# Attention and two feed-forward layers on one core: the fifth pair's scores traced after the fourth pair's output, first loads on two queues, first head's operands moved by engines and second's by DMA

## The chip, the core and the metric

The kernel runs on one core of a Trainium2 chip. The core has a matrix engine (PE), three elementwise engines (DVE, ACT, POOL) and queues that start DMAs; SP's queue (SPq in the rows) does nothing else, ACT's queue can start DMAs too. Every engine and every queue works through its own list of instructions in order and waits where an input or a buffer is not ready. The metric is the device time of one execution in microseconds.

## What is computed

```python
# q, k, v: (4, 8, 576, 64); x: (2304, 512); d_ff = 2048
scores = q @ k.transpose(0, 1, 3, 2) / 8
scores = where(scores >= max(scores) - tau, scores, -1e9)   # per row
attn   = softmax(scores) @ v                                # (4, 8, 576, 64)
x = attn.transpose(0, 2, 1, 3).reshape(2304, 512)
x = (s * relu(x @ w_in) ** 2 + b) @ w_out                   # moe
h = x @ w2_in                                               # moe2
out = (h * tanh(softplus(h))) @ w2_out
```

## The kernel before

**Attention** works on 16 pairs of heads (4 batches of 4 pairs), each in 9 tiles of 128 query rows. `load_raw` reads q, k and v of a pair, 12 DMAs, all on SP's queue. `prep_qk` transposes q or k on PE (5 transposes, line 206), splits it into a rounded part `hi` (ACT, line 210) and a remainder `lo` (DVE, line 211), and puts these into the operand tiles Q, KH[h], KL[h] by `move`: for the first pair with copies on ACT, DVE and POOL (lines 230 to 234), for the others with DMAs on SP's queue (line 228, 12 for a pair). The tiles `hi` and `lo` have one buffer each, so q's parts wait until k's moves have read theirs.

`scores` makes one tile: 4 matmuls (8 for tile 4, which holds rows of both heads) into a tile S, the scaled copy with row minimum on DVE (`ns`, line 258), the exponential on ACT (line 265) and, by the returned function `finish`, the threshold and row sum on DVE (line 269) and the normalisation on POOL (line 279). `weights_t` transposes the normalised rows (T, lines 291 to 300) and copies them out on ACT (`te`, line 302); `product` multiplies them with v (line 313); `split_x` reads the result of a pair out on ACT and DVE (lines 321, 322) and makes it `x[pair]`.

**Order.** `attention` is a generator. Its step k traces the scores of tile k, the preparation of the next pair at tiles 2 and 4, then `weights_t` of tile k - 7, then `product` of the tile before. So x[3], the last output of the first batch, is traced in step 43, after 8 score tiles of the fifth pair (pair 4, counted from 0). `run` calls this generator alone until x[3] exists, with one step of `w1` (the splitting of the first layer's weights from 64 to 32 bits, `split_w`, lines 59 to 72) for every 12 yields. Then it closes the second buffer of S and gives its PSUM to `mm`, the accumulators of `moe1`, and interleaves attention with `moe1(0)`, `moe1(1)` and `moe1(2)` by planned costs; there attention is traced with a priority that puts it 200 places ahead. `moe1(b)` needs x[4b] to x[4b+3]; its groups are lines 405 (matmuls h and y). `moe1(0)` takes its weights from `w1`, through a ring of 5 units. `moe1(3)` runs with the splitting of the second layer's weights (line 59 again), and `moe2` closes the kernel.

The traced order is a priority, not the order of execution: a planner (`schedule_with_timeline_sim=True`) goes through the traced instructions and puts each on its engine's list when its inputs and buffers are ready by its own costs, lowest priority number first.

Of the kernel before, what the change touches and what calls it, by code (L numbers as in the profile page):

```python
# [8 lines left out]
F32 = mybir.dt.float32  # L9
F32R = mybir.dt.float32r  # L10
# [5 lines left out]
P = 128  # L16
# [3 lines left out]
class Fused:  # L20
# [113 lines left out]
    def attn_alloc(self):  # L134
        nc = self.nc
        self.sets = []

        e4 = self.at.tile([P, 1344], F32, name="E4", bufs=1)
        for g in range(3):
            nc.gpsimd.memset(e4[:, g * 640:g * 640 + 64], 0.0)  # L140
        for g in range(2):

            Q = self.at.tile([P, 1216], F32R, name=f"Q{g}", bufs=1)
            nc.gpsimd.memset(Q[:, 576:640].bitcast(F32), 0.0)
            KH = [self.at.tile([P, 576], F32R, name=f"KH{g}{h}", bufs=1) for h in range(2)]

            KL = [self.at.tile([P, 576], F32R, name=f"KL{g}{h}", bufs=1) for h in range(2)]
            for h in range(2):
                nc.gpsimd.memset(KL[h][HALVES[1 - h], :].bitcast(F32), 0.0)
            self.sets.append((Q, KH, KL, e4[:, g * 640:g * 640 + 704]))  # L150
        self.qk = {}
        for n in "qk":
            t = self.qk[n] = self.at.tile([P, 5, 2, 64], F32, name=f"raw{n}", bufs=1)
            nc.gpsimd.memset(t[64:128, 4], 0.0)
        self.vs = []
        for g in range(2):
            t = self.at.tile([P, 2, 5, 64], F32, name=f"rawv{g}", bufs=1)
            nc.gpsimd.memset(t[64:128, 0, 4, :], 0.0)
            nc.gpsimd.memset(t[0:64, 1, 4, :], 0.0)
            self.vs.append(t)  # L160

    def load_raw(self, pr, nm):
        nc = self.nc
        b, p = divmod(pr, self.NP)
        if b >= self.B:
            return
        src = {"q": self.q, "k": self.k, "v": self.v}[nm]
        h2 = src[b, 2 * p:2 * p + 2]
        rem = h2[:, 512:576, :].rearrange("h r d -> r h d")
        if nm == "v":  # L170
            t = self.vs[pr % 2]
            for h in range(2):
                nc.sync.dma_start(t[:, h, 0:4, :], h2[h, 64 * h:64 * h + 512, :].rearrange("(p c) d -> p c d", c=4))
            nc.sync.dma_start(t[0:64, 0, 4, :], h2[0, 512:576, :])
            nc.sync.dma_start(t[64:128, 1, 4, :], h2[1, 0:64, :])
        else:
            t = self.qk[nm]
            nc.sync.dma_start(t[:, 0:4, 0, :], h2[0, 0:512, :].rearrange("(p c) d -> p c d", c=4))
            if nm == "q":
                nc.sync.dma_start(t[:, 0:4, 1, :], h2[1, 0:512, :].rearrange("(p c) d -> p c d", c=4))  # L180
                nc.sync.dma_start(t[0:64, 4, :, :], rem)
            else:


                full = h2[1, 64:576, :].rearrange("(p c) d -> p c d", c=4)
                nc.sync.dma_start(t[64:128, 0:4, 1, :], full[0:64])
                nc.sync.dma_start(t[0:64, 1:5, 1, :], full[64:128])
                nc.sync.dma_start(t[0:64, 0, 1, :], h2[1, 0:64, :])
                nc.sync.dma_start(t[0:64, 4, 0, :], h2[0, 512:576, :])
        self.raws[pr, nm] = t  # L190

# [3 lines left out]
        pool = self.s2p if self.s2p and self.n_s % 2 else self.sp  # L195
        return pool.tile([P, 1024], F32, tag="S", name=name)

    def prep_qk(self, pr, n):


        nc = self.nc
        raw = self.raws.pop((pr, n))
        Q, KH, KL, _ = self.sets[pr % 2]
        tp = self.s_tile(f"tp{n}{pr}")
        for c in range(5):
            nc.tensor.transpose(tp[:, c * 128:c * 128 + 128], raw[:, c].rearrange("p h d -> p (h d)"), self.ident)
        self.load_raw(pr + 1, n)
        hi = self.at.tile([P, 576], F32R, tag="hi", name=f"hi{n}{pr}", bufs=1)
        lo = self.at.tile([P, 576], F32R, tag="lo", name=f"lo{n}{pr}", bufs=1)
        nc.scalar.copy(hi, tp[:, :576])  # L210
        nc.vector.tensor_tensor(lo, tp[:, :576], hi.bitcast(F32), op=ALU.subtract)
        for h, (own, oth) in enumerate((HALVES, HALVES[::-1])):
            for half, t in ((own, hi), (oth, hi if n == "k" else lo)):
                if n == "k":
                    parts = [(KH[h], 0, 576, 0)]
                else:
                    parts = [(Q, 0, 576, 0)] if h == 0 else [(Q, 0, 512, 704), (Q, 512, 576, 128)]
                for dst, a, z, o in parts:
                    self.move(pr, dst[half, a + o:z + o], t[own, a:z], t is hi)
            if n == "k":  # L220
                self.move(pr, KL[h][own, :], lo[own, :], None)

    def move(self, pr, dst, src, early):


        nc = self.nc
        if pr:
            nc.sync.dma_start(dst.bitcast(F32), src.bitcast(F32))
        elif early is None:
            nc.gpsimd.tensor_copy(dst, src.bitcast(F32))  # L230
        elif early and dst.shape[-1] > 64:
            nc.scalar.copy(dst, src.bitcast(F32))
        else:
            nc.vector.tensor_copy(dst, src.bitcast(F32))

# [88 lines left out]
    def attention(self):  # L326

        nc = self.nc  # L330
        N = 9 * self.B * self.NP
        LAG = 7
        for n in "kq":
            self.load_raw(0, n)
        nc.sync.dma_start(self.tau_c, self.tau.partition_broadcast(P))
        nc.sync.dma_start(self.s_c, self.s.partition_broadcast(P))
        nc.sync.dma_start(self.b_c, self.b.partition_broadcast(P))
        self.load_raw(0, "v")
        for n in "kq":
            self.prep_qk(0, n)  # L340
        fin = todo = None
        tes = {}
        for k in range(N + LAG + 2):
            pr, ti = divmod(k, 9)
            if k < N:
                nxt = self.scores(pr, ti)
                if fin:
                    fin()
                fin = nxt
                yield 550  # L350
                if pr + 1 < self.B * self.NP and ti in (2, 4, 8):
                    if ti == 8:
                        self.load_raw(pr + 1, "v")
                    else:
                        self.prep_qk(pr + 1, "kq"[ti // 2 - 1])
                        yield 500
            elif fin:
                fin()
                fin = None
            j = k - LAG  # L360
            if 0 <= j < N:
                prj, ci = divmod(j, 9)
                tnew = self.weights_t(prj, ci)
                yield 550
            if todo:
                tp, tc, te = todo
                tes[tc] = te
                if tc == 4:
                    self.product(tp, 4, (te, te), True, False)
                    yield 490  # L370
                elif tc > 4:
                    self.product(tp, tc - 5, (tes[tc - 5], te), False, tc == 8)
                    yield 970
                if tc == 8:
                    self.split_x(tp)
            todo = (prj, ci, tnew) if 0 <= j < N else None


    def acc(self, name):
# [204 lines left out]
    def run(self, ctx):  # L584
# [8 lines left out]
        m, a = ExitStack(), ExitStack()  # L593
# [16 lines left out]
        k = 0  # L610
        while 3 not in self.x:
            next(att)
            k += 1
            if k % 12 == 0:
                next(w1)

        pro.close()
# [23 lines left out]
        while a_on or m_on:  # L641
            if a_on and (not m_on or (a_done - 5000.0) / a_left <= m_done / m_left):
                with tc.high_priority(offset=200):
                    c = next(att, None)
                a_on = c is not None
                a_done += c or 0
            else:
                c = next(mo, None)
# [23 lines left out]
HALVES = [slice(0, 64), slice(64, 128)]  # L672
# [45 lines left out]
```

## Time and profile before

| | us |
|---|---|
| three runs | 1215.17, 1219.55, 1219.41 (median 1219.41) |
| the profiled execution | 1216.89, its span 1215.1 |
| attention alone, to the first matmul of `moe1(0)` | 131.47 |
| attention with `moe1(0)` | 132 to 356 |
| attention with `moe1(1)` and `moe1(2)` | 356 to 664 |
| `moe1(3)` and the splitting of the second layer | 664 to 830 |
| `moe2` | 830 to 1215 |

A row of a timeline is start, duration, engine, line, operation, written tile <- read tile, shapes and a count; square brackets hold the idle time of the engine before the row and what ended it. Times are microseconds from the first instruction. A row of a table by stretches gives each engine's busy time with the number of its instructions, then the granted clock of PE as a share of full speed.

### The profile page before, as it was taken

To read this page: it belongs to the slowest core of one execution; us is meant where nothing else is said; L and a number is where in the kernel's file an instruction comes from. 1 tells how busy PE (TensorE), PEld (TensorE's weight loads), DVE (VectorE), ACT (ScalarE), POOL (GpSimd) and SP (SyncE) were. 2 spreads that over 40 slices of the span, in tenths; PEclk is the share of its full clock that TensorE was granted. 3 is DMA by queue.
4 is the path that set the end of the run, shared out by engine and by line. 5 is a ranking of instruction groups with operands and counts; after the bars stand their busy time and mean duration, and the time that the engine had idled before them with its cause. 6 is when DMAs were issued, how large, how long until landed. Compare 5 with 4: busy or idle time off the path is not lost.

```text
span 1215.1 us, 20290 instructions
## 1 busy us (share of the span) xinstructions
PE 1153.1 (95%) x7104; PEld 983.9 (81%) x7104; DVE 868.4 (71%) x1585; ACT 592.5 (49%) x1153; POOL 657.9 (54%) x841
## 2 busy tenths in 40 slices
PE   5888999999899999999999999988999999999998
PEld 4666878877788998988998999966888888888886
DVE  5888777878885465664652799799977676767865
ACT  4666666575555544455532575453433333344332
POOL 5566777786644343335431354346755655555654
PEclk8989999999999999999999999989999999999999
DMA  5556466576585445474433898842130020020000
GB/s 129 157 142 180 111 210 183 168 208 175 175 288 165 144 144 165 127 227 132 131 99 111 288 323 267 293 148 70 36 104 1 1 70 1 8 97 1 18 1 35
DMA packets 123671, 161.88 MB, mean 133 GB/s; under 512 B 57392, under 2 KB 78896, under 8 KB 123568
## 3 DMA queue, kind: packets, MB, share of 16 engines
q1 hardware_dynamic: 123568, 160.58, 43.2%
q8 instruction: 56, 0.92, 0.3%
q14 instruction: 47, 0.39, 0.1%
HBM read 107.48 MB, written 30.93 MB: 114 GB/s over the span
## 4 chain that ended last, share of the span: by engine, by line
PE 59%; DVE 13%; DMA 10%; POOL 6%; issue 5%; ACT 4%; SPq 2%; DVEq 0%; ACTq 0%; POOLq 0%
PE o L539 12%; PE h L405 11%; PE y L405 9%; PE pv L313 6%; PE hp L495 6%; PE hm L495 6%; PE S L254 5%; DMA wraw<-in_moe_w_in_dram 5%; PE T L291 4%; DMA wraw<-in_moe_w_out_dram 3%; DVE d L512 3%; POOL e L279 2%; DVE wa L67 2%; DVE wa L68 2%; DVE wa L66 2%
## 5 line engine op out<-in xcount | busy, mean ns | idle before, releaser
L512 DVE RECIPROCAL d<-d 128x512 f32<-128x512 f32 (+1 forms) x80 | 242.0, 3025 | 0.0
L405 PE MATMUL y<-gh,w 128*128 128x288 f32 x768 | 164.0, 299 | 2.7 <-DVE y L452 2.7
L405 PE MATMUL h<-xh,w 128*128 128x288 f32 x768 | 164.8, 300 | 1.3 <-DMA w<-w 1.0
L269 DVE SCALAR_TENSOR_TENSOR e<-ns,st,e 128x576 f32<-128x576 f32 x128 | 120.9, 948 | 45.5 <-ACT e L265 30.1
L260 POOL TENSOR_SCALAR st<-st,tau_c 128x1 f32<-128x1 f32 x144 | 60.9, 424 | 165.9 <-DVE ns L258 151.0
L539 PE MATMUL o<-w2o,g2h 128*128 128x512 f32 x576 | 149.7, 395 | 0.1
L258 DVE TENSOR_SCALAR_CACHE_REDUCE ns<-S 128x576 f32<-128x576 f32 x144 | 107.8, 752 | 55.6 <-PE S L254 54.9
L279 POOL TENSOR_SCALAR e<-e,st 128x576 f32<-128x576 f32 x128 | 126.4, 997 | 31.3 <-DVE st L274 28.9
L405 PEld LDWEIGHTS y<-gh,w 128*128 128x128 f32 x768 | 125.7, 188 | 10.2 <-issue 4.4
L265 ACT ACTIVATE e<-ns,st 128x576 f32<-128x576 f32 x128 | 98.9, 776 | 70.6 <-DVE ns L258 59.5
L405 PEld LDWEIGHTS h<-xh,w 128*128 128x128 f32 x768 | 125.7, 188 | 8.5 <-issue 5.7
L539 PEld LDWEIGHTS o<-w2o,g2h 128*128 128x128 f32 x576 | 107.1, 188 | 24.8 <-ACT g2h L519 0.6
L302 ACT COPY te<-T 128x576 f32<-128x576 f32 x144 | 91.3, 634 | 72.1 <-PE T L296 64.9
L429 POOL TENSOR_TENSOR gl<-rr,gh 128x288 fp32r<-128x288 f32 x96 | 81.0, 850 | 73.8 <-DVE rr L428 63.2
L495 PE MATMUL hp<-y,w2i 128*128 128x512 f32 (+1 forms) x480 | 113.6, 380 | 6.1 <-DVE t L511 6.0
L516 POOL TENSOR_TENSOR t<-t,d 128x512 f32<-128x512 f32 (+1 forms) x80 | 94.9, 1186 | 40.5 <-DVE d L512 40.3
L523 POOL TENSOR_TENSOR g2l<-t,g2h 128x512 fp32r<-128x512 f32 (+1 forms) x80 | 95.5, 1193 | 38.4 <-ACT g2h L519 36.1
L405 PE MATMUL y<-gl,w 128*128 128x288 f32 x384 | 113.7, 296 | 1.5 <-DVE gl L429 1.5
L405 PE MATMUL h<-xl,w 128*128 128x288 f32 x384 | 113.8, 296 | 0.0
L495 PE MATMUL hm<-y,w2i 128*128 128x512 f32 (+1 forms) x480 | 110.1, 373 | 3.1 <-DVE t L511 3.0
L254 PE MATMUL S<-KH,Q 128*128 128x288 f32 x320 | 101.6, 333 | 11.8 <-DVE ns L258 4.0
L291 PE MATMUL T<-ident,e 128*128 128x128 f32 x576 | 99.1, 281 | 13.6 <-ACT te L302 9.3
(100 smaller groups left out, 2481.8 us busy)
## 6 DMA issues: line engine op xcount, KB each, us to landing
w<-w SPq DMA_DIRECT2D x96, 512.0 KB, 4.2
wraw<-in_moe_w_in_dram SPq DMA_DIRECT2D x64, 256.0 KB, 3.9
w<-wp SPq DMA_DIRECT2D x32, 512.0 KB, 4.0
wraw<-in_moe_w_out_dram SPq DMA_DIRECT2D x64, 256.0 KB, 4.3
KH<-hik SPq DMA_DIRECT2D x60, 144.0 KB, 2.5
y<-yT SPq DMA_DIRECT2D x32, 256.0 KB, 4.1
KL<-lok SPq DMA_DIRECT2D x30, 144.0 KB, 2.7
rawq<-in_q_dram SPq DMA_DIRECT2D x32, 128.0 KB, 3.1
```

Of the source, the lines that this page charges most:

```text
L254: nc.tensor.matmul(so, Q[:, c0:c0 + 128], kt[:, ks], start=(i == 0), stop=(i == len(terms) - 1))
L258: nc.vector.tensor_scalar(ns.rearrange("p (h n) -> p h n", h=2), sv, -0.125, 3.0e38, op0=ALU.mult, op1=ALU.min, accum_out=nm[:, c1])
L265: nc.scalar.activation(e, ns, AF.Exp, bias=nm[:, c1], scale=-1.0)
L269: nc.vector.scalar_tensor_tensor(e, ns, nthr[:, c1], e, op0=ALU.is_le, op1=ALU.mult, accum_out=sm[:, c1])
L279: nc.gpsimd.tensor_scalar(t, t, rinv[:, j:j + 1], u[:, j:j + 1], op0=ALU.mult, op1=ALU.add)
L291: nc.tensor.transpose(T[:, i * 128:i * 128 + 128], self.es[pr, i, "pair"][:, o:o + 128], self.ident)
L405: nc.tensor.matmul(acc[:, :n], w[:, wl, c], rhs[c][xl][:, ts], start=(i == 0), stop=(i == 11))
L495: nc.tensor.matmul(hp[:, :n], w[:, wl, kc, fs], yy[kc], start=(i == 0), stop=(i == 11))
L512: nc.vector.reciprocal(d, d)
L516: nc.gpsimd.tensor_tensor(t, t, d, op=ALU.mult)
L523: nc.gpsimd.tensor_tensor(gl, t, gh.bitcast(F32), op=ALU.subtract)
L539: nc.tensor.matmul(outs[t], g[:, t * 128:t * 128 + 128], w[:, wl, fc % 4, :], start=(fc == 0 and i == 0), stop=(fc == 15 and i == 2))
```

## The change

Four things are changed. In `attention`, the scores of pair 4 are not traced until x[3] exists: from tile 36 on (9 tiles by 4 pairs) the loop goes on with `weights_t` and `product` alone, without the lag of 7, until `split_x(3)` is traced, and takes up the scores then; from there the lag of 7 is built up anew. In `load_raw`, for the first pair, the second head's loads of k (3) and q (1) go to ACT's queue. The first pair is prepared by `prep_first`: k and q are transposed one behind the other, q's parts get buffers of their own (tag `te`), the first head's operands are copied by ACT, POOL and DVE, and the second head's (3 for k, 4 for q) are moved by DMAs on SP's queue. The zeroing of the raw tiles moves to the head of POOL's list, and `w1` takes a step for every 16 yields in place of 12.

```diff
 load_raw:
+        other = nc.sync if pr else nc.scalar
...
-                nc.sync.dma_start(t[:, 0:4, 1, :], h2[1, 0:512, :].rearrange("(p c) d -> p c d", c=4))
+                other.dma_start(t[:, 0:4, 1, :], h2[1, 0:512, :].rearrange("(p c) d -> p c d", c=4))
...
-                nc.sync.dma_start(t[64:128, 0:4, 1, :], full[0:64])
-                nc.sync.dma_start(t[0:64, 1:5, 1, :], full[64:128])
-                nc.sync.dma_start(t[0:64, 0, 1, :], h2[1, 0:64, :])
+                other.dma_start(t[64:128, 0:4, 1, :], full[0:64])
+                other.dma_start(t[0:64, 1:5, 1, :], full[64:128])
+                other.dma_start(t[0:64, 0, 1, :], h2[1, 0:64, :])
...
+    def prep_first(self):
+        nc = self.nc
+        tps = [self.raw_t(0, n) for n in "kq"]
+        (kh, kl), (qh, ql) = (self.parts(0, n, tp, tags) for n, tp, tags in
+                              zip("kq", tps, (("hi", "lo"), ("te", "te"))))
+        k0, k1, k2 = self.moves(0, "k", 0, kh, kl)
+        q0, q1 = self.moves(0, "q", 0, qh, ql)
+        nc.scalar.copy(k0[0], k0[1].bitcast(F32))
+        nc.gpsimd.tensor_copy(k1[0], k1[1].bitcast(F32))
+        nc.gpsimd.tensor_copy(k2[0], k2[1].bitcast(F32))
+        nc.scalar.copy(q0[0], q0[1].bitcast(F32))
+        nc.vector.tensor_copy(q1[0], q1[1].bitcast(F32))
+        for n, hi, lo in (("k", kh, kl), ("q", qh, ql)):
+            for dst, src in self.moves(0, n, 1, hi, lo):
+                nc.sync.dma_start(dst.bitcast(F32), src.bitcast(F32))
...
 attention:
-        for k in range(N + LAG + 2):
-            pr, ti = divmod(k, 9)
-            if k < N:
+        s = t = 0
+        while s < N or t < N or todo:
+            on = s < N and not (s == 9 * self.NP and self.NP - 1 not in self.x)
+            if on:
+                pr, ti = divmod(s, 9)
+                s += 1
...
-            j = k - LAG
-            if 0 <= j < N:
-                prj, ci = divmod(j, 9)
-                tnew = self.weights_t(prj, ci)
+            new = None
+            if t < s - LAG or (t < s and not on):
+                prj, ci = divmod(t, 9)
+                t += 1
+                new = prj, ci, self.weights_t(prj, ci)
...
 run:
-            if k % 12 == 0:
+            if k % 16 == 0:
```

`raw_t`, `parts` and `moves` are `prep_qk` cut into three: the transposes with the next pair's load, the two parts, and the list of moves for one head. In `moves` a head of k has three entries (KH twice, KL once), the first head of q two, the second head of q four.

## Rows read from the trace of the kernel before

**Rows 1.** Table of engines on the page: busy us, share of span, instructions.
```profile
PE 1153.1 (95%) x7104; PEld 983.9 (81%) x7104; DVE 868.4 (71%) x1585; ACT 592.5 (49%) x1153; POOL 657.9 (54%) x841
```

**Rows 2.** Busy time by stretches: stretch, length; busy (instructions) of PE, PEld, DVE, ACT, POOL; clock, DMA.
```profile
12.00:101.00 89.00, 73.88 (x426) 54.61 (x427) 73.57 (x206) 50.44 (x88) 54.53 (x73) 0.88 0.58 151
101.00:132.00 31.00, 28.21 (x191) 20.84 (x190) 25.34 (x73) 20.34 (x35) 16.45 (x26) 0.94 0.63 169
132.00:356.00 224.00, 209.26 (x1472) 179.26 (x1470) 176.25 (x439) 136.73 (x287) 160.80 (x227) 0.98 0.63 188
356.00:510.00 154.00, 153.94 (x1147) 139.43 (x1148) 85.18 (x214) 75.63 (x142) 67.33 (x95) 1.00 0.53 158
664.00:830.00 166.00, 154.63 (x1034) 145.00 (x1033) 141.76 (x295) 89.67 (x222) 70.37 (x73) 0.98 0.74 248
```

**Rows 3.** Timeline of the start, all engines.
```profile
4.71 0.63 SPq L180 DMA_DIRECT2D rawq<-in_q_dram  x1
...
5.08 1.30 PE L206 MATMUL tpk<-ident,rawk 128*128 128x128 f32 x5 [5.08 <-DMA rawk<-in_k_dram]
...
7.09 2.71 ACT L232 CAST KH<-hik 64x576 fp32r<-64x576 f32 x4
...
7.92 1.30 PE L206 MATMUL tpq<-ident,rawq 128*128 128x128 f32 x5 [1.54 <-DMA rawq<-in_q_dram]
...
11.52 1.01 DVE L234 CAST Q<-loq 64x576 fp32r<-64x576 f32 x3
...
12.12 0.58 PE L254 MATMUL S<-KH,Q 128*128 128x288 f32 x1 [2.90 <-DVE Q L234]
```

**Rows 4.** Timeline of SP's queue, and of ACT and PE where they wait, 18 to 33 us.
```profile
18.13 0.43 ACT L64 ACTIVATE wraw<-wraw 128x256 f32<-128x256 f32 x1 [2.13 <-DMA wraw<-in_moe_w_in_dram]
...
20.07 1.20 SPq L228 DMA_DIRECT2D KH<-hik  x2
...
27.86 0.61 PE L254 MATMUL S<-KH,Q 128*128 128x288 f32 x1 [1.33 <-DVE loq L211]
...
32.21 1.61 SPq L59 DMA_DIRECT2D wraw<-in_moe_w_in_dram  x3
```

**Rows 5.** View of waits, 0 to 131 us: total, times, longest.
```profile
ACT hiq L210 <- DMA KH<-hik: 0.9, 1, 0.9
```

**Rows 6.** Timeline of PE from the last score tile of pair 3 to `moe1(0)`.
```profile
100.66 0.40 PE L254 MATMUL S<-KH,Q 128*128 128x288 f32 x1
...
103.06 0.40 PE L254 MATMUL S<-KH,Q 128*128 128x288 f32 x1
...
103.69 0.60 PE L291 MATMUL T<-ident,e 128*128 128x128 f32 x4
...
127.33 0.60 PE L291 MATMUL T<-ident,e 128*128 128x128 f32 x4
127.77 0.27 PE L296 MATMUL T<-ident,E 128*128 128x128 f32 x1
127.97 1.19 PE L313 MATMUL pv<-te,rawv 128*64 128x288 f32 x8
129.09 0.40 PE L254 MATMUL S<-KH,Q 128*128 128x288 f32 x1
...
131.47 0.41 PE L405 MATMUL h<-xh,wp 128*128 128x288 f32 x1
```

**Rows 7.** Timeline of ACT, a copy of T in that stretch.
```profile
128.13 0.64 ACT L302 COPY te<-T 128x576 f32<-128x576 f32 x1 [0.39 <-PE T L296]
```

**Rows 8.** Timeline of DVE, one score tile's two passes.
```profile
128.65 0.75 DVE L258 TENSOR_SCALAR_CACHE_REDUCE ns<-S 128x576 f32<-128x576 f32 x1
...
130.60 0.81 DVE L269 SCALAR_TENSOR_TENSOR e<-ns,st,e 128x576 f32<-128x576 f32 x1
```

**Rows 9.** Timeline of POOL, tenth and next splitting of a piece of `w1`.
```profile
97.93 1.19 POOL L72 TENSOR_TENSOR wp<-wa,wp 128x256 fp32r<-128x256 f32 x1 [0.25 <-ACT wp L71]
...
139.04 1.43 POOL L72 TENSOR_TENSOR wp<-wa,wp 128x256 fp32r<-128x256 f32 x2
```

More of the change, by code (lines that the diff above doesn't have):

```diff
@@ L136, in attn_alloc @@
         self.sets = []
+        self.qk = {}
+        for n in "kq":
+            t = self.qk[n] = self.at.tile([P, 5, 2, 64], F32, name=f"raw{n}", bufs=1)
+            nc.gpsimd.memset(t[64:128, 4], 0.0)
         e4 = self.at.tile([P, 1344], F32, name="E4", bufs=1)
@@ L150, in attn_alloc @@
             self.sets.append((Q, KH, KL, e4[:, g * 640:g * 640 + 704]))
[L151 to L154, printed above, removed]
         self.vs = []
@@ L196, in s_tile, with raw_t @@
         return pool.tile([P, 1024], F32, tag="S", name=name)
-    def prep_qk(self, pr, n):
+    def raw_t(self, pr, n):
         nc = self.nc
         raw = self.raws.pop((pr, n))
-        Q, KH, KL, _ = self.sets[pr % 2]
         tp = self.s_tile(f"tp{n}{pr}")
@@ L207, in prep_qk, with parts @@
         self.load_raw(pr + 1, n)
-        hi = self.at.tile([P, 576], F32R, tag="hi", name=f"hi{n}{pr}", bufs=1)
-        lo = self.at.tile([P, 576], F32R, tag="lo", name=f"lo{n}{pr}", bufs=1)
+        return tp
+    def parts(self, pr, n, tp, tags):
+        nc = self.nc
+        hi, lo = (self.at.tile([P, 576], F32R, tag=t, name=f"{w}{n}{pr}", bufs=6 if t == "te" else 1)
+                  for w, t in zip(("hi", "lo"), tags))
         nc.scalar.copy(hi, tp[:, :576])
         nc.vector.tensor_tensor(lo, tp[:, :576], hi.bitcast(F32), op=ALU.subtract)
[L212 to L219, printed above, removed]
-            if n == "k":
-                self.move(pr, KL[h][own, :], lo[own, :], None)
@@ L223, in move, with moves @@
-    def move(self, pr, dst, src, early):
-        nc = self.nc
[L227 to L234, printed above, removed]
+        return hi, lo
+    def moves(self, pr, n, h, hi, lo):
+        Q, KH, KL, _ = self.sets[pr % 2]
+        own, oth = HALVES[h], HALVES[1 - h]
+        out = []
+        for half, t in ((own, hi), (oth, hi if n == "k" else lo)):
+            if n == "k":
+                spans = [(KH[h], 0, 576, 0)]
+            else:
+                spans = [(Q, 0, 576, 0)] if h == 0 else [(Q, 0, 512, 704), (Q, 512, 576, 128)]
+            out += [(dst[half, a + o:z + o], t[own, a:z]) for dst, a, z, o in spans]
+        return out + ([(KL[h][own, :], lo[own, :])] if n == "k" else [])
@@ new lines, in prep_qk @@
+    def prep_qk(self, pr, n):
+        hi, lo = self.parts(pr, n, self.raw_t(pr, n), ("hi", "lo"))
+        for h in range(2):
+            for dst, src in self.moves(pr, n, h, hi, lo):
+                self.nc.sync.dma_start(dst.bitcast(F32), src.bitcast(F32))
+    def prep_first(self):
+        nc = self.nc
+        tps = [self.raw_t(0, n) for n in "kq"]
[11 more added lines that the diff above has]
+                nc.sync.dma_start(dst.bitcast(F32), src.bitcast(F32))
@@ L338, in attention @@
         self.load_raw(0, "v")
-        for n in "kq":
-            self.prep_qk(0, n)
+        self.prep_first()
         fin = todo = None
         tes = {}
-        for k in range(N + LAG + 2):
-            pr, ti = divmod(k, 9)
-            if k < N:
+        s = t = 0
[4 more added lines that the diff above has]
+                s += 1
                 nxt = self.scores(pr, ti)
@@ L375, in attention @@
                     self.split_x(tp)
-            todo = (prj, ci, tnew) if 0 <= j < N else None
+            todo = new
     def acc(self, name):
```

## The prediction

> **What bounds the kernel now.** I read the page's table of engines first: PE is busy for 95% of the span [rows 1], so a change pays only where PE loses time. The busy times by stretches [rows 2] show where that is. With `moe1(1)` PE is busy for 153.94 of 154 us and starts 1147 instructions, one in 0.134 us; time moved into such a stretch comes back one to one. In attention alone it is busy for 73.88 of 89 us with a clock of 0.88 (12 to 101) and for 28.21 of 31 with 0.94 (101 to 132). Here DVE is the fullest engine: 73.57 of 89 and 25.34 of 31. With `moe1(0)` PE still idles for 14.7 of 224 us, and that stretch takes 70 us longer than the next one; DVE is busy for 79% of it. I then read the start row by row [rows 3 to 5], and the end of attention alone [rows 6 to 8].
>
> What a score tile costs: on PE 103.69 - 103.06 = 0.63 us [rows 6] (0.53 more for the tile of both heads), on DVE 0.75 + 0.81 = 1.56 us [rows 8]. What the rest of a tile costs on PE: T from 127.33 to 127.97, 0.64 us, and pv from there to 129.09, 1.12 us [rows 6]. A product is made for 5 of 9 tiles.
>
> **The start.** Before, the transposes of q wait for the load of q's second head, whose issue begins at 4.71 as the seventh of SP's list, and start at 7.92; the first score tile starts at 12.12 and had waited for DVE's three copies of q (11.52, 1.01 us) [rows 3]. Of SP's first eight loads four go to ACT's queue. By SP's 0.63 us for an issue [rows 3], q's second head comes out some 4.71 - 2.6 = 2.1 us earlier, if ACT's queue starts at once. Of the eight copies on ACT and DVE, two by ACT and one by DVE stay: ACT's four for k take 2.71 us, so a copy costs about 0.68. With these together I work out 2.8 us for the first score tile, at 9.3. The zeroing of the raw tiles hides either way, since it was done before the first transposes at 5.08.
>
> Against this stands SP's list. The second head's seven moves are new on it: 7 x 0.6 (KH's two took 1.20 [rows 4]) = 4.2 us, less 4 x 0.63 = 2.5 for the loads that left, a net 1.7 us. They pass in front of pair 1's moves, which were issued from 20.07 on, and of the weights' loads; SP's list is full until the three loads at 32.21 in the timeline. Who waits for that: `hi` has one buffer, so pair 1's `hi` of q waits for its moves of k [rows 5], DVE's `lo` follows it, and at 27.86 a score tile waits for that `lo` 1.33 us, since it needs the S buffer [rows 4]. So the eighth tile hangs on SP's list, not on the first tile's start. Nothing before shows the new order, so I bound it: from 2.8 us gained (SP's moves slip into gaps) to 1.7 lost. I take 1.0 gained, between the ends but nearer to the gain's side, because ACT also loses 2.13 us at 18.13 in waiting for a weight load [rows 4], which the later steps of `w1` may spare.
>
> The Trainium skill speaks against a larger gain ("DMA: Bandwidth & Descriptors", section "Issuing engines are not separate DMA queues"): a second issuing engine saves only the time of initiating, all transfers share the same engines. No row of this trace has loads on two queues; by that rule the 2.1 us above are all that the second queue can give, and the sum stays as it is.
>
> **`w1` for every 16 yields.** Nothing. Its steps in attention alone fall from 9 to 6, but the trace has run ahead of the traced order all along (the tenth piece was split at 97.93, where the traced order had finished some three, and the next only at 139.04 [rows 9]: ten pieces fill the ring of 5 units), so buffers set its pace, and DVE's share of it moves little. If that cover is gone, `moe1(0)` starts with three units where it had five; two units are 48 matmuls, 48 x 0.134 = 6.4 us, which is in the range.
>
> **The end of attention alone.** The last tile of pair 3 starts at 100.66, and `moe1(0)` at 131.47 [rows 6]: 30.8 us. In between stand 11 T, 9 of pair 3 and 2 of pair 2, with 8 products (3 of pair 2, 5 of pair 3), and 11 score tiles: the nine of pair 4 and two of pair 5. Without these, T and te alternate: 0.64 on PE, 0.64 on ACT [rows 7], and about 0.2 between (127.97 to 128.13), which is 1.5 us for a tile without product; with one, pv covers te and a tile takes 0.64 + 1.12 = 1.76. The first two tiles and the last five of pair 3 have one, the other four don't: 7 x 1.76 + 4 x 1.5 = 18.3, and the last product 1.1: 19.4 us. `moe1(0)` so starts 30.8 - 19.4 = 11.4 us earlier. POOL's normalisation of the last four tiles is needed only after six T, some 9 us on, and is done by then.
>
> What leaves this stretch comes back where PE is full: 11 x 0.63 + 0.53 = 7.5 us of scores, ten transposes (the next pair's k and q) at (127.77 - 127.33) / 4 = 0.11, 1.1, and T of (4,0), 0.64 [rows 6]: 9.2 us. The net is 2.2 us gained. PE's loss in the 30.8 us is 30.8 - (11 x 0.64 + 8 x 1.12 + 9.2) = 30.8 - 25.2 = 5.6 us; more than that can't be won here, and it is won if scores fill all gaps of the shorter chain. So the gain is between 0 (nothing moves) and 5.6. I take 2.2, which needs no gap to be filled.
>
> **The restart.** Pair 4 now begins with nothing in flight: nine score tiles go through DVE before its first T. That is 9 x 1.56 = 14.0 us of DVE work, which sat in attention alone, in the stretch with `moe1(0)`, where DVE is busy for 176.25 of 224 us and splits the weights that PE waits for. DVE's idle 48 us hide it, if it lands there; I take 0.5 us lost, and bound it by 0 and by the rival below. x[3] comes 12 us earlier, which is about the time of these nine tiles, so the last output of attention keeps its distance from `moe1(3)`.
>
> **The sum.** 1216.89 - 1.0 - 2.2 + 0.5 = 1214.2 for an execution like the profiled one. That one lies 2.5 us under the median of the runs, 1219.41, so the median would be 1216.7; I put the forecast at 1215, between the two.
>
> **Rivals.** First, the planner undoes the change. The traced order is a priority only: the score tile at 129.09 is one of pair 5, which was traced after x[3], and it ran before it [rows 6]. With 200 places of priority ahead, pair 4's tiles can run amid pair 3's T as they did. Then only the start is left, -1.0: 1215.9, and 1218.4 on the median. Against it: S(4,0) itself, and the rest for as long as the S buffer is taken.
>
> Second, all gaps are filled: the start gives its 2.8 and the chain its 5.6, with nothing lost at the restart: 1216.89 - 8.4 = 1208.5, 1211.0 on the median. For it speaks that ACT and DVE have slack once the scores no longer stand in front.
>
> Third, the other side: DVE paces the stretch with `moe1(0)`. If the nine score tiles, pair 5's preparation (two DVE passes of 0.75) and the rest of what moved, some 17 us, take room at DVE's 79%, the stretch grows by 17 / 0.79 = 21.5 us and not by 9.2: 1216.89 - 1.0 - 11.4 + 21.5 = 1226.0, 1228.5 on the median. It decides from a growth of some 18.5 us on. For it speaks that this stretch is 70 us longer than the next one and PE idles in it; against it that PE is busy in it for 93%.
>
> **Chances.** A difference of 0.5%, 6.1 us, is about what a measurement of this kernel tells from none. The forecast has 0.36, of which 0.06 falls under 1213.3, the bound of faster. The planner undoing it has 0.15, all within 0.5%. All gaps filled has 0.29, faster. DVE pacing the stretch has 0.20, slower. So faster 0.35, within 0.45, slower 0.20. The range takes in most of the second and of the third rival and the unknown ends of the start: 1204 to 1229.
>
> **What would show it.** In the timeline of the start: the first score tile near 9.3 (right) or past 11; the eighth tile before 27 or after 28. At the end of attention alone: `moe1(0)` at 118 to 121, no score tile of pair 4 between the last T of pair 3 for the forecast, and many for the first rival. In the busy times by stretches: `moe1(0)`'s stretch longer by about 9 us. The prediction is wrong if that stretch grows by more than 18, or if PE's clock falls in the thinner chain of T and te, or if the later stretches, which are untouched, move by more than 2 us.

## The result and the profile after

The changed kernel takes 1231.26 us (median of 8, 1225.23 to 1235.29) against 1219.29 beside it: ratio 1.0102, interval 1.0075 to 1.0128. The forecast was 1215.0 in 1204 to 1229, no measurable change; the kernel is slower, and its time lies above the range. The profiled execution took 1228.97 us, its span is 1227.2.

Table of engines of the changed kernel (answers [rows 1]), then its busy times by stretches (columns as in [rows 2]):

```profile
PE 1156.2 (94%) x7104; PEld 988.9 (81%) x7104; DVE 869.3 (71%) x1582; ACT 589.5 (48%) x1149; POOL 661.8 (54%) x841
```

```profile
12.00:101.00 89.00, 72.33 (x419) 54.92 (x420) 71.30 (x203) 50.91 (x87) 54.23 (x72) 0.85 0.62 159
101.00:132.00 31.00, 28.09 (x191) 20.72 (x190) 20.73 (x58) 17.04 (x29) 17.22 (x22) 0.94 0.50 133
132.00:356.00 224.00, 202.09 (x1401) 172.55 (x1399) 177.52 (x431) 131.72 (x282) 157.23 (x224) 0.98 0.59 180
356.00:510.00 154.00, 150.00 (x1100) 134.30 (x1099) 84.06 (x214) 76.56 (x139) 60.25 (x89) 0.99 0.55 164
...
330.00:356.00 26.00, 23.21 (x144) 19.48 (x145) 21.82 (x61) 13.18 (x24) 14.98 (x18) 0.87 0.59 177
356.00:370.00 14.00, 11.19 (x76) 8.32 (x74) 10.95 (x29) 8.42 (x13) 5.59 (x8) 1.00 0.73 212
```

The amount of work is the same; what differs is how much PE has started by a given time. Against [rows 2] it is 7 instructions behind in 12 to 101, level in 101 to 132, 71 behind in 132 to 356 and 47 in 356 to 510: 125 instructions of 0.134 us, 16.8 us, of which 12.1 are left at the end of the span. The two narrow rows show the thickest piece: from 330 to 370 us 220 instructions start. In the kernel before it is 287 (first two rows; the others are x[8] and the handover from `moe1(0)` to `moe1(1)` in the kernel before):

```profile
330.00:356.00 26.00, 25.20 (x180) 20.83 (x178) 23.11 (x60) 14.21 (x25) 9.88 (x13) 1.00 0.88 270
356.00:370.00 14.00, 13.94 (x107) 13.36 (x108) 10.29 (x27) 9.17 (x19) 11.26 (x14) 1.00 0.72 251
...
348.42 0.63 ACT L321 CAST xh<-pv 128x576 fp32r<-128x576 f32 x1
...
351.84 2.47 SPq L397 DMA_DIRECT2D w<-w  x5
...
356.06 0.40 PE L405 MATMUL h<-xh,w 128*128 128x288 f32 x1 [0.44 <-DMA w<-w]
```

Timelines of the changed kernel: the start (answers [rows 3]), the end of attention alone (answers [rows 6]), and the handover from `moe1(0)` to `moe1(1)`, with SP's queue, PE and x[8] (ACT):

```profile
0.72 0.65 ACTq L187 DMA_DIRECT2D rawk<-in_k_dram  x1
...
6.13 1.27 PE L204 MATMUL tpq<-ident,rawq 128*128 128x128 f32 x5
...
9.67 0.82 PE L273 MATMUL S<-KH,Q 128*128 128x288 f32 x2 [2.27 <-DVE Q L250]
...
27.34 0.61 PE L273 MATMUL S<-KH,Q 128*128 128x288 f32 x1
...
108.23 0.40 PE L428 MATMUL h<-xh,wp 128*128 128x288 f32 x1
...
109.93 0.29 PE L273 MATMUL S<-KH,Q 128*128 128x288 f32 x1
...
130.16 0.40 PE L273 MATMUL S<-KH,Q 128*128 128x288 f32 x1
...
132.66 0.64 ACT L340 CAST xh<-pv 128x576 fp32r<-128x576 f32 x1 [0.48 <-PE pv L332]
...
356.75 0.30 PE L428 MATMUL y<-gh,wp 128*128 128x290 f32 x1
...
360.11 0.56 SPq L235 DMA_DIRECT2D Q<-hiq  x1
...
361.74 0.62 ACT L340 CAST xh<-pv 128x576 fp32r<-128x576 f32 x1
...
366.03 0.38 SPq L486 DMA_DIRECT2D yT<-yl  x1
...
367.24 2.83 SPq L420 DMA_DIRECT2D w<-w  x5
...
371.33 0.47 PE L428 MATMUL h<-xh,w 128*128 128x288 f32 x1 [1.19 <-DMA w<-w]
```

The first score tile comes 2.45 us earlier than before, the eighth 0.52. x[3] is read out at 132.66 (131.86 before): seven of pair 4's score tiles (the row at 109.93 is the third, that at 130.16 the last) still run amid pair 3's T, although they are traced behind x[3]. `moe1(0)` has 18 matmuls from 108.23 on and then waits for x[3]. At 350 us `moe1` is hardly behind the kernel before, with 31.0 and 31.7 of its units of 24 matmuls; what is behind is attention: x[8] is read out at 361.74, before at 348.42. At the handover `moe1(1)` starts 14.6 us after the last y of `moe1(0)`: its weight loads (L420, issued from 367.24 on) stand in SP's list behind the loads and moves of an attention pair and the last y's stores. In the kernel before they were issued at 351.84, ahead of those stores, and `moe1(1)` started at 356.06, 4 us after the last y.

PE's waits, 132 to 375 us (total, times, longest), of the changed kernel, then the same three of e3 (the first experiment), the fastest of the kernels below:

```profile
PE S L273 <- DVE ns L277: 9.7, 7, 3.3
PE T L310 <- ACT te L321: 4.4, 7, 1.6
PE T L310 <- POOL e L298: 3.2, 5, 1.1
```

```profile
PE S L273 <- DVE ns L277: 0.6, 1, 0.6
PE T L310 <- ACT te L321: 1.6, 3, 1.1
PE T L310 <- POOL e L298: 0.7, 2, 0.5
```

So PE loses 17.3 us here and 2.9 in e3 to attention's own chain of scores and weights; directly for the pieces of `w1` (`wp`) it waits 2.5 and 1.5 us.

### The profile page after: what moved, and what is told of

It is laid out like the page before. It is cut to its first block, busy times and chain, and to the rows that moved or that the text cites. A ratio compares the mean times of both kernels' runs of the same rounds, so it can differ in the third digit from the quotient of the medians.

```text
span 1227.2 us, 20273 instructions
## 1 busy us (share of the span) xinstructions
PE 1156.2 (94%) x7104; PEld 988.9 (81%) x7104; DVE 869.3 (71%) x1582; ACT 589.5 (48%) x1149; POOL 661.8 (54%) x841
## 4 chain that ended last, share of the span: by engine, by line
PE 60%; DVE 15%; DMA 9%; issue 6%; POOL 6%; ACT 3%; SPq 1%; DVEq 0%; ACTq 0%; POOLq 0%
PE o L562 12%; PE h L428 11%; PE y L428 9%; PE pv L332 6%; PE hp L518 6%; PE hm L518 5%; PE S L273 5%; PE T L310 4%; DMA wraw<-in_moe_w_out_dram 3%; DMA wraw<-in_moe_w_in_dram 3%; DVE d L535 3%; DVE wa L67 2%; DVE wa L68 2%; DVE wa L66 2%; POOL e L298 2%
## 5 line engine op out<-in xcount | busy, mean ns | idle before, releaser
L288 DVE SCALAR_TENSOR_TENSOR e<-ns,st,e 128x576 f32<-128x576 f32 x128 | 117.2, 918 | 47.9 <-ACT e L284 30.4
L298 POOL TENSOR_SCALAR e<-e,st 128x576 f32<-128x576 f32 x128 | 129.8, 1022 | 33.5 <-DVE st L293 29.0
L279 POOL TENSOR_SCALAR st<-st,tau_c 128x1 f32<-128x1 f32 x144 | 57.6, 400 | 155.9 <-DVE ns L277 140.2
L310 PE MATMUL T<-ident,e 128*128 128x128 f32 x576 | 100.0, 282 | 17.3 <-ACT te L321 10.0
```

Of the source, the lines that this page charges most:

```text
L288: nc.vector.scalar_tensor_tensor(e, ns, nthr[:, c1], e, op0=ALU.is_le, op1=ALU.mult, accum_out=sm[:, c1])
L298: nc.gpsimd.tensor_scalar(t, t, rinv[:, j:j + 1], u[:, j:j + 1], op0=ALU.mult, op1=ALU.add)
L310: nc.tensor.transpose(T[:, i * 128:i * 128 + 128], self.es[pr, i, "pair"][:, o:o + 128], self.ident)
```

## The experiments

A stands for: SP's list at the handover is the cause. B: DVE paces the stretch with `moe1(0)`. C: the pace of `w1` starves `moe1(0)`, by its lead (C1, the number of steps before `moe1(0)`) or its density (C2). D: the new first preparation is to blame. R: each edit is first of all another order of the planner's, and the order sets the time. Other letters are explained where they come. Ratios are to the kernel before on the same chip, with 95% intervals. "The order" is the list in which the planner put the instructions of an engine.

**1. One part alone, and the change without its new pace.**

```diff
 e1, attention (the kernel before):
-        for k in range(N + LAG + 2):
+        while s < N or t < N or todo:
+            on = s < N and not (s == 9 * self.NP and self.NP - 1 not in self.x)
...
 e2, attention (the kernel before; with the new load_raw and attn_alloc):
-        for n in "kq":
-            self.prep_qk(0, n)
+        self.prep_first()
```

> The kernel before with the new loop of attention alone (pair 4's scores traced after x[3]); the old first preparation, all first loads on SP, a step of w1 for every 12 yields. Theory A (order of SP's list: moe1(1)'s weight loads stood behind the last y stores of moe1(0), issued at 367.24 us, and cost the 15 us without moe1 work from 356.75 to 371.33): the deferral itself costs little, and since the planner puts these loads in front of the last stores here, the time is 1217 to 1222. Theory B (DVE paces the stretch with moe1(0) after the deferral, rival 3 of the prediction): about 1229 to 1233. Theory C (the pace of w1, 16 in place of 12, is to blame): 1217 to 1221. Theory D (the new first preparation is to blame): 1217 to 1221.

> The kernel before with the new first preparation alone (second queue for four first loads, first head's operands by engines, second head's by DMA); the old loop of attention and 12 yields. Theory A: the first score tile comes 2.4 us earlier and the gain is lost again by pair 0's second head: 1217 to 1220. Theory B and C: the same, 1217 to 1220. Theory D (seven more DMAs on SP's list at the start disturb what follows): 1228 to 1233.

```diff
 run (e3: the changed kernel with the old pace):
-            if k % 16 == 0:
+            if k % 12 == 0:
                 next(w1)
```

> The changed kernel with a step of w1 for every 12 yields again, nothing else. Theory A: the planner puts the first weight loads of moe1(1) ahead of the last y stores of moe1(0) here too, so the gap at the handover closes: 1217 to 1222. Theory B: 1229 to 1233, as DVE has the same work. Theory C: 1217 to 1221, and then the units of moe1(0) lie ahead of those of the changed kernel by 132 us already. Theory D: 1229 to 1233.

Measured: deferral alone 1217.11 us, 0.9992 (0.9971 to 1.0013); first preparation alone 1218.31, 0.9998 (0.9979 to 1.0017); both, with a step for every 12 yields, 1213.49, 0.9959 (0.9941 to 0.9978), which is faster than the kernel before. B and D fall. The forecasts of A and C for e3 were too high, and C's side claim failed: by 130 us e3 has as much of `moe1(0)` as the changed kernel, 0.8 units; at 350 us it has 36.2 units of `moe1` against 31.0. The orders of e1 and e3 are nearly one (laid side by side, 59 of the 7,104 entries of PE's list differ), so their 3.6 us are about what the first preparation is worth in that order: x[3] comes at 126.95 in e3 and 131.3 in e1. Busy times of e3:

```profile
132.00:356.00 224.00, 213.78 (x1505) 183.16 (x1503) 185.27 (x436) 136.32 (x295) 165.54 (x230) 1.00 0.65 201
...
330.00:356.00 26.00, 26.00 (x193) 22.82 (x192) 16.89 (x37) 14.17 (x31) 15.19 (x20) 1.00 0.74 236
```

DVE does more here than in the changed kernel (185.27 against 177.52), and PE starts 104 instructions more: DVE was not full, it stood idle behind others.

**2. The pace with the other parts: the eight combinations.**

```diff
 run (e7: the kernel before; e16: with the deferral; e17: with the first preparation):
-            if k % 12 == 0:
+            if k % 16 == 0:
                 next(w1)
```

> The kernel before with a step of w1 for every 16 yields, nothing else: 7 steps before moe1(0) in place of 9. Theories C1 and C2: slower than before, 1223 to 1231. Theory A (SP's list at the handover is that of the kernel before): 1215 to 1220. Theory E (it is the combination with the deferral, which takes 11 of the 112 yields away, that falls below what moe1(0) needs): 1215 to 1222.

> The kernel before with the new loop of attention alone and a step of w1 for every 16 yields, with the old first preparation: the cell that is missing beside 12 with the deferral (ratio 0.9992) and 16 alone (1.0015). If the loss is one of these two parts together, 1226 to 1233. If all three parts are needed, or by theory R an order of its own: 1213 to 1225.

> The kernel before with the new first preparation and a step of w1 for every 16 yields, with the old loop of attention: the last missing cell of the eight (before 1, deferral 0.9992, first preparation 0.9998, sixteen 1.0015, deferral and first preparation 0.9959, deferral and sixteen 1.0029, all three 1.0102). If the first preparation and sixteen together bring the loss: 1224 to 1233. If only all three do (theory R, an order of its own): 1214 to 1222.

Measured: sixteen alone 1216.92, 1.0015 (1.0001 to 1.0029); with the deferral 1219.82, 1.0029 (1.0012 to 1.0047); with the first preparation 1215.66, 0.9983 (0.9966 to 0.9999). No single part and no two cost over 0.3%; only all three together do, 1.0102. C1 and C2 missed e7. E met it; but E lays the loss on the pace with the deferral, and e16, which has just these two, costs 0.3%.

**3. Is it the pace, or the order that it tips?**

```diff
 run (the changed kernel):
-            if k % 16 == 0:
+            if k % 12 == 0 and k <= 72:      # e5; e8: k % 8, e14: k % 24, e15: k % 14
                 next(w1)
+        next(w1)                             # e6 alone: with k % 16, two steps
+        next(w1)                             # behind the loop
```

> The changed kernel with a step of w1 for every 12 yields, but none after the sixth: as many steps before moe1(0) as in the changed kernel (6; 8 in the run with 12, which took 1213.5 us), laid as densely as with 12. Theory C1 (what counts is the lead, the number of steps traced before moe1(0), since moe1(0) then takes one step for every two of its own): 1227 to 1233. Theory C2 (what counts is how densely the steps are laid while attention is alone): 1211 to 1216. Theory A (the order of SP's list at the handover to moe1(1); the planner puts its first weight loads ahead of the third y's stores here, as with 12): 1212 to 1219.

> The changed kernel (a step of w1 for every 16 yields) with two more steps right before moe1(0), so eight in all. Theory C1 (the lead): 1211 to 1216, like the run with 12. Theory C2 (the density): 1227 to 1233. Theory A (SP's list: two weight loads of moe1(1) stand ahead of the last y's stores here, the third behind them): between the two, 1220 to 1228.

> The changed kernel with a step of w1 for every 8 yields: 12 steps before moe1(0). Theory C1 (the lead): not slower than the run with 12, 1208 to 1214. Theory C2 (the density): the same, or slower if the steps now take DVE and ACT from attention alone, 1211 to 1220. Theory A (SP's list as in the run with 12): 1211 to 1217. Theory R (every other order is a new draw, without a trend): anywhere from 1212 to 1231.

> The changed kernel with a step of w1 for every 24 yields: 4 steps before moe1(0) in place of 6. PE and POOL run the very order of the changed kernel, the other engines but for ten neighbours. Theory R (what costs is the planner's order, to which the number of steps matters only where it tips it): the time of the changed kernel, 1227 to 1234. Theories C1 and C2 (fewer or thinner steps starve moe1(0)): slower still, 1235 to 1245.

> The changed kernel with a step of w1 for every 14 yields (7 steps); the planner's order differs from that of 12 and from that of 16. Theories C1 and C2: between the two, 1218 to 1227. Theory R: a new draw, 1212 to 1231. Theory A (the first weight load of moe1(1) stands before the last y's stores in SP's list here, the second and the rest behind them): 1224 to 1231.

| | steps before `moe1(0)` | us | ratio (interval) |
|---|---|---|---|
| e8, every 8 | 12 | 1221.46 | 1.0042 (1.0027 to 1.0058) |
| e3, every 12 | 8 | 1213.49 | 0.9959 (0.9941 to 0.9978) |
| e5, every 12, six | 6 | 1214.70 | 0.9980 (0.9969 to 0.9991) |
| e15, every 14 | 7 | 1225.75 | 1.0079 (1.0057 to 1.0101) |
| e6, every 16 and two | 8 | 1224.26 | 1.0057 (1.0035 to 1.0079) |
| changed, every 16 | 6 | 1231.26 | 1.0102 (1.0075 to 1.0128) |
| e14, every 24 | 4 | 1227.48 | 1.0095 (1.0074 to 1.0116) |

Neither the number of steps nor their density goes with the time: e5 has the changed kernel's six steps and is 1.2% faster, e6 has e3's eight and is 1% slower, e8 has most and is slower than e3. The order does. Every kernel of the table runs the same instructions on PE, ACT, DVE and POOL; PE's order is entry for entry the same in e3 and e5, and again the same in the changed kernel and e14, and these two pairs have close times. Between 16 and 24 the pace changes nothing; between 12 and 16 it tips the planner into other orders, from the places of the first raw pieces on; of PE's lists of e3 and the changed kernel 1,206 of the 7,104 entries differ, laid side by side. Another order is not a loss as such: e1's list for PE differs from that of the kernel before in 1,087 entries, and the time is the same. C1 missed e5, e6 and e8, C2 e6 and e8, both missed e14 and both met e15; A missed e8 (1211 to 1217). R's range held wherever it was given here, but it is 7 to 19 us wide and tests little.

**4. What the bad order loses at the handover.**

```diff
 moe1, unit (the changed kernel):
+            with self.tc.high_priority(offset=400):
                 nc.sync.dma_start(w.bitcast(F32), self.w1s[key])
```

> The changed kernel with the weight loads of moe1(1) to moe1(3) traced with 400 places of priority ahead, nothing else. In SP's list the first three then stand after the first y tile's stores of moe1(0) and not behind the last. Theory A: moe1(1) starts within 3 us of the last y of moe1(0), and not 15 us after it; PE had only attention's work in that gap and made 76 instructions in 14 us (107 before), so the gain is 5 to 10 us: 1221 to 1226. Theories B, C and D: the gap closes, but attention, which ran in it, is late instead, and the time stays at 1229 to 1233.

Measured 1225.73, 1.0068 (1.0044 to 1.0091). The orders of PE, ACT, DVE and POOL are those of the changed kernel up to the last y of `moe1(0)` (PE's first 2,030 matmuls), so this run isolates the handover. It closes: three loads go out at 345.86, and `moe1(1)` starts at 359.50, 0.13 us after the last y.

```profile
330.00:356.00 26.00, 21.27 (x125) 18.06 (x126) 22.05 (x61) 12.63 (x24) 15.11 (x17) 0.87 0.59 178
356.00:370.00 14.00, 14.00 (x101) 11.16 (x100) 7.14 (x18) 7.18 (x13) 5.14 (x7) 1.00 0.94 300
...
345.86 1.56 SPq L421 DMA_DIRECT2D w<-w  x3
...
359.50 0.30 PE L429 MATMUL h<-xh,w 128*128 128x288 f32 x1
```

Of the 25 starts that PE wins behind 356 it misses 19 ahead of it; the rest of the gain shows behind 370 (1046 starts to 510 us against 1026). By the medians of the ratios the gap was worth 0.34%, some 4 us, a third of the loss against the kernel before; but the two intervals overlap, so the closing of the gap is shown and its worth is not. A can hold for about a third, the rest lies elsewhere: e4 is still slower than the kernel before.

**5. Are late raw weight pieces the rest?** Theory W: the order issues them late, and ACT, whose list is in order, stands before them. Waits for raw pieces, 132 to 345 us, first of the changed kernel, then of e3:

```profile
ACT wraw L64 <- DMA wraw<-in_moe_w_out_dram: 19.3, 18, 3.6
ACT wraw L64 <- DMA wraw<-in_moe_w_in_dram: 12.8, 14, 3.1
DVE wa L66 <- ACT wraw L64: 10.6, 7, 2.5
```

```profile
ACT wraw L64 <- DMA wraw<-in_moe_w_out_dram: 17.2, 20, 3.6
ACT wraw L64 <- DMA wraw<-in_moe_w_in_dram: 7.9, 13, 1.4
DVE wa L66 <- ACT wraw L64: 4.6, 6, 1.5
```

```diff
 run, weights_t and, for te, parts (e9 the changed kernel, e10 that with 12, e11 the kernel before; e12: te alone):
-                            self.pre, ("raw", "ra"), bufs=3)
+                            self.pre, ("raw", "ra"), bufs=4)
-        te = self.at.tile([P, 576], F32, tag="te", name=f"te{pr}_{ci}", bufs=6)
+        te = self.at.tile([P, 576], F32, tag="te", name=f"te{pr}_{ci}", bufs=5)
```

> The changed kernel with four buffers for the raw weight pieces in place of three; to make room the copies te have five buffers in place of six. Theory W (moe1(0) goes at the pace of the weights' split, and in the changed kernel the raw pieces land late: between 132 and 345 us ACT waits 32.1 us for loads of raw pieces and DVE 10.6 us for the ACT pass behind them, against 25.1 and 4.6 in the run with a step for every 12 yields): a fourth buffer lets a load be issued a piece earlier, some 3.7 us, so that these waits fall under 25 together, and the time to 1211 to 1219. Theory R (each edit is a new draw of the planner's order, and the waits for raw pieces do not set the time): 1214 to 1231 without any tie to these waits. Theory A (SP's list at the handover alone): the first weight load of moe1(1) stands before the last y's stores here, the others behind most of them: 1222 to 1227.

> The same two buffer counts in the changed kernel with a step of w1 for every 12 yields (1213.5 us with three raw buffers). Theory W: the waits for raw pieces (29.7 us together with three buffers) fall under 20, and the time to 1206 to 1212; the difference to the changed kernel with four buffers is under 5 us. Theory R: 1208 to 1225, and the difference between the two is as likely to be over 5 us as under it.

> The same two buffer counts in the kernel before (33.2 us of such waits with three buffers). Theory W: 1207 to 1214, as moe1(0) gets its weights earlier. Theory R: 1210 to 1225.

> The changed kernel with five buffers for te alone, as a control for the room that the fourth raw buffer took. Theory W: te's buffers play no part, and the waits for raw pieces stay near 40 us: 1228 to 1234. Theory R: a new draw, 1214 to 1231.

| | waits for raw pieces, us | us | ratio (interval) |
|---|---|---|---|
| e9, changed, four raw | 26.7 (42.7 with three) | 1215.80 | 1.0000 (0.9987 to 1.0014) |
| e10, with 12, four raw | 22.8 (29.7) | 1218.28 | 1.0015 (1.0000 to 1.0030) |
| e11, before, four raw | 27.8 (33.2) | 1214.09 | 0.9981 (0.9968 to 0.9994) |
| e12, changed, te five | 36.9 (42.7) | 1218.80 | 1.0009 (0.9989 to 1.0029) |

The waits fall, if not as far as W said (under 25 and under 20), but the time doesn't follow: e10 has the shortest and is slower than e3, e12, which only takes a buffer away, wins 0.9% with most of the waits left, and e14, with the changed kernel's order and nearly its time, has 31.4 us of them, about as e3. W falls as the cause. A misses e9. In e12 1,098 entries of PE's list differ from the changed kernel; an edit that takes a buffer away and still gives back nearly the whole loss is the plainest sign for R.

**6. The deferral as it was meant.** In all kernels so far the planner ran score tiles of pair 4 ahead of x[3]. Here a dependency forbids it.

```diff
 attention (e3, ahead of pair 4's first scores):
+                if s == 9 * self.NP + 1:
+                    z = self.at.tile([P, 1], F32, name="gate", bufs=1)
+                    nc.gpsimd.tensor_scalar(z, self.x[3][1][:, 0:1].bitcast(F32), 0.0, None, op0=ALU.mult)
+                    k0 = self.sets[0][1][0][:, 0:1]
+                    nc.gpsimd.tensor_tensor(k0, k0.bitcast(F32), z, op=ALU.add)
```

> The changed kernel with a step of w1 for every 12 yields (1213.5 us), and pair 4's scores made to depend on x[3]: two one-column POOL passes multiply a column of x[3] by zero and add it to the first column of pair 4's KH, so that the planner can't run these scores ahead. Theory P (the prediction's working: the end of attention alone is shorter by 11.4 us without these scores, and 9.2 us of PE work come back later): x[3] comes at 115 to 119 us in place of 127.0, pair 4's scores all stand behind it, and the time is 1209 to 1213.5. Theory S (the scores ran in gaps of the chain of T and te, and pair 4 restarted with nothing in flight is late for good): x[3] comes at 119 to 124, x[4] later than 168.0 by 5 us or more, and the time is 1217 to 1226. Theory R (an edit is first of all a new order): x[3] earlier, and the time anywhere from 1212 to 1226.

e18 has `self.x[2]` in place of `self.x[3]`:

> The kernel of the forced deferral (1234.4 us) with the same two POOL passes, but its column taken from x[2] and not from x[3]: the control for these passes, and a smaller dose of the deferral (in the planner's order some five of pair 4's score tiles then stand ahead of x[3], none did). If what costs in the forced deferral is that DVE has no score tile for 15 us (111.8 to 126.7) and PE's clock falls to 0.50 there (107 to 120): no such hole, x[4] within 8 us of 168.0, and the time 1212 to 1222. If the passes themselves or their place in the order cost: 1229 to 1235.

Measured: forced 1234.44, 1.0150 (1.0135 to 1.0166), 20.9 us more than e3; with x[2] 1223.44, 1.0047 (1.0030 to 1.0064). Timeline of e13's PE (T without a product), ACT (a copy `te` and what stood ahead of it, x[3], x[4]) and DVE, then two such T and x[4] of e3, then e13's busy times, then those of e3:

```profile
105.14 0.66 PE L310 MATMUL T<-ident,e 128*128 128x128 f32 x4 [0.98 <-ACT te L321]
...
106.56 0.44 ACT L64 ACTIVATE wraw<-wraw 128x256 f32<-128x256 f32 x1 [0.94 <-DMA wraw<-in_moe_w_in_dram]
106.91 0.62 ACT L321 COPY te<-T 128x576 f32<-128x576 f32 x1
...
107.58 1.12 PE L310 MATMUL T<-ident,e 128*128 128x128 f32 x4 [1.67 <-ACT te L321]
...
109.63 1.12 PE L310 MATMUL T<-ident,e 128*128 128x128 f32 x4 [0.73 <-ACT te L321]
...
126.06 0.64 ACT L340 CAST xh<-pv 128x576 fp32r<-128x576 f32 x1 [1.39 <-PE pv L332]
...
126.73 0.76 DVE L341 TENSOR_TENSOR xl<-pv,xh 128x576 fp32r<-128x576 f32 x1 [14.92 <-ACT xh L340]
...
208.55 0.63 ACT L340 CAST xh<-pv 128x576 fp32r<-128x576 f32 x1
```

```profile
109.85 0.66 PE L310 MATMUL T<-ident,e 128*128 128x128 f32 x4 [0.89 <-ACT te L321]
...
111.34 0.66 PE L310 MATMUL T<-ident,e 128*128 128x128 f32 x4 [0.73 <-ACT te L321]
...
168.00 0.63 ACT L340 CAST xh<-pv 128x576 fp32r<-128x576 f32 x1
```

```profile
101.00:107.00 6.00, 3.72 (x24) 1.92 (x24) 4.99 (x15) 3.75 (x8) 2.67 (x6) 0.99 0.77 260
107.00:120.00 13.00, 10.15 (x40) 6.67 (x42) 3.25 (x7) 5.02 (x11) 3.57 (x4) 0.50 0.30 105
```

```profile
101.00:107.00 6.00, 6.00 (x41) 4.40 (x41) 4.92 (x13) 4.22 (x7) 2.69 (x5) 1.00 0.73 249
107.00:120.00 13.00, 10.62 (x77) 8.21 (x77) 11.32 (x31) 7.82 (x14) 8.93 (x10) 1.00 0.40 102
```

No score tile of pair 4 stands ahead of x[3] any more, and x[3] comes only 0.9 us earlier than in e3 (126.06, 126.95). A tile of the chain of T and te takes 1.49 us in e3 at full clock, as the prediction had it; in e13 it takes 2.44 and then 2.05. The 2.44 come from ACT, whose list has the splitting of a raw weight piece ahead of the copy: it waits 0.94 us for that piece. The 2.05 come with PE's granted clock at 0.50, its lower level, for 13 us from about 107 on (T takes 1.12 us in place of 0.66). DVE, whose work the scores are, has nothing to do for 14.92 us, and x[4] comes at 208.55 against 168.00. From 12 to 370 us PE starts 2082 instructions against 2240 in e3: 158 x 0.134 = 21.2 us, the loss. P falls; S had the sign, but its times for x[3] and the end were too good, and R's 1212 to 1226 was missed too. The control e18 keeps four tiles ahead of x[3] (e3 six): clock 0.74 from 107 to 120, x[4] at 182.43 (14 us later than in e3, where I expected 8 at most) and half of the loss, more than I expected. With the same two passes the kernel loses 10 us to e3 with x[2] and 21 with x[3], so some 11 of the 21 go with the dose, if their orders cost alike; how much of e18's own 10 us is its order is open. What the clock and what the hole in DVE's work cost was not told apart. The Trainium skill describes such a fall ("TensorE: Matmul & The Clock Gate", section "HAM oscillation — how this bites in real kernels") for short bursts of matmuls between longer waits for DMA. The rows show it with waits for ACT's copies, none over 1.67 us: 0.99, then 0.50.

## Why the prediction was wrong, step by step

**The start**, 1.0 us gained: the mechanism held for the first tile; the size depends on the order. The first score tile came at 9.67 (9.3 worked out), the eighth at 27.34, between "right" and "wrong". In like orders (e1, e3) the part is worth 3.6 us, in the order of e2 nothing. q's transposes start 1.79 us earlier (6.13, 7.92 before) for the 2.1 that the second queue was given, as the Trainium skill's rule quoted there would have it.

**`w1` for every 16 yields**, "Nothing": this step failed. Its cover was real: up to 132 us ten pieces are split with 12 (e3), with 16 and even with 24 (e14), and 16 alone costs 0.15% (e7). But I priced the pieces only, and took the prices of the parts to add up, when each edit also makes the planner choose another order. With the other two parts the same edit takes the ratio from 0.9959 to 1.0102, some 17 us: the two others together had won 5, and 12 are lost in the end.

**The end of attention alone**, 2.2 us gained: the step did not take place. (A row was misread besides: the tile at 100.66 is the last but one of pair 3, the last starts at 103.06 [rows 6]. So nine tiles of pair 4 and one of pair 5 follow, not two; both terms shrink by 0.6 us, the net stays.) x[3] and the start of `moe1(0)` in earnest stayed at 132 us, as the first rival said (chance 0.15). That rival was right in its mechanism and wrong in its time: "only the start is left" took for granted that an order that looks the same up to 132 us goes on the same. Where the step is forced, its working fails in two terms: a tile of the bare chain takes 2.05 to 2.44 us and not 1.5, with PE's clock at its lower level and ACT's copies behind a late weight piece, and what I let come back "where PE is full" as 9.2 us comes back as a hole in DVE's work. The prediction named a falling clock in this chain as a sign against it, but priced none; the trace of the kernel before already had it there, at 0.51 from 114 to 117 us:

```profile
113.66 1.12 PE L291 MATMUL T<-ident,e 128*128 128x128 f32 x4 [1.43 <-ACT te L302]
```

**The restart**, 0.5 us lost: mis-sized for a deferral that is kept. There x[4] comes 40 us later and the kernel loses 21 us to e3 (e13), though the runs don't split this between the restart and the slow chain ahead of it. In the changed kernel, where seven tiles ran ahead, x[4] came at 175.01, 172.27 before.

**The third rival** gave 1226.0 to 1228.5, near the time by luck, for a reason that isn't there: DVE is busy for 177.52 of 224 us (176.25 before), and where it does more, in e3, the kernel is faster. The stretch with `moe1(0)` grows, but because engines wait for each other in a worse order.

**What stays open.** R says that the order sets the time. e5 and e14 show it, by the same lists at another pace and nearly the same times, and e12 fits it; the handover (e4) may be a third of the loss. In the rest PE waits for attention's scores and weights (17.3 us, 2.9 in e3), and e14, with the same order, shows 16.4. Which entries of the order bring these waits about between 132 and 330 us was not settled.

## What to carry to other kernels

With a planner between the traced program and the lists, an edit has two prices: its own, and that of the new order; here the second was worth up to 17 us, and edits without a price of their own tipped it. So measure each part alone and together, compare the lists of the engines, and read nothing into one variant's time under 1% before a neutral edit has shown the spread. Work that seems to stand in front of a critical chain may be what keeps PE's clock up and DVE fed: look at which engine idles once it is gone.

## What the runs showed of the chip

Between e3 and the changed kernel nothing differs but the places of `w1`'s steps in the traced order; at 350 us PE is five units of `moe1` further in e3 (36.2, 31.0). And in e13 PE's granted clock fell to 0.50 for 13 us after waits of no more than 1.67 us between T tiles of two thirds of a microsecond; in e3, with waits of 0.89 and 0.73 us in the same chain and other matmuls between, it stayed at 1.00.
